# A fifth tile of at most 64 tokens: 16 second products instead of 24, and a second scatter that adds

## The chip, the cores and the metric

The kernel runs on one core of a Trainium2 chip. Its engines each work through their own list of instructions in order: TensorE (PE in the profile, its weight loads PEld), VectorE (DVE), ScalarE (ACT), GpSimd (POOL) and SyncE (SP, which here only issues DMAs). They wait for one another through semaphores. The metric is the device time of one execution in microseconds (us), the median of several runs. Before the change it is 557.7 us (three runs, 557.35 to 557.83).

## The reference

Retention over 8 batches, 8 heads, 576 positions and a head size of 64 gives `x`, 4608 tokens of 512 numbers. Each token then goes to one of eight experts:

```python
logits = xn @ en.T / tau                   # x and the expert embeddings, normalised
expert_idx = np.argmax(logits, axis=1)
gate_w = probs[np.arange(N), expert_idx]
for e in range(E):                         # E = 8, D = 512, F = 1024
    mask = expert_idx == e
    h = np.maximum(x[mask] @ w1[e], 0.0)
    out[mask] = gate_w[mask, None] * (h @ w2[e])
```

How many tokens an expert gets is known only on the chip.

## The kernel before, in words

The kernel first computes the retention and, beside it, a table that gives each expert 640 slots: five tiles of 128. `gid` holds for each slot the token whose row is gathered, `sid` the token whose row is written (a number out of range, 1e6, for an empty slot, which the scatter skips). Slots of one tile lie in an order of halves: the first of two tokens at column c of the left 64, the second at column c of the right 64. So a fifth tile with at most 64 tokens fills the first 32 columns of each half.

Numbers are float32, and each operand of the experts' products is kept as a high and a low part (`fp32r`). A product is made of three passes: high by high, high by low and low by high. From line 577 to the end of the experts all engines keep the order in which the code is written.

Each expert e from 1 to 7 goes through two stages:

- the **first products** (`x @ w1`, line 1224): seven products of blocks instead of eight, for each of four quarters i, 28 in all, in the order of the table `ORDER` (lines 1267 to 1271). A product is written (n, i). It is six matmuls of 288, 304 or 320 columns, chosen on PE by a branch on `rest[e]`, the number of tokens in the fifth tile (at most 64, at most 96, more). After each product `follow` copies and adds the bank: ACT copies `Y[i]` after n = 1, 6 and 7 into one of the five tiles `ys` (line 1248), and the next product that adds into `Y[i]` waits for that copy. `settle` turns the sums into the high part of `hs` (ACT, line 1193) and the low part (DVE, line 1186).
- the **second products** (`h @ w2`, line 1302): for each of the five tiles 24 matmuls of 512 columns (eight blocks of h times three passes) into one bank. ACT scales the bank by the gate into `ys[i]` (line 1314), and POOL scatters the 128 rows to `out` (line 1276). The fifth tile of experts 1 to 6 stands under `tc.If(rest[e] > 0)`, on PE alone: without tokens its matmuls are jumped over.

Beside these, tables of tasks (`mm1_plan`, `mm2_plan`) say after which product or tile ACT, DVE and POOL prepare what comes next: `xjoin`, `xsums`, `xhigh`, `xlow` turn the next expert's gathered tokens into its operands `xsa` and `xsb` (ACT line 446, DVE line 450), `w1hi` and `w1lo` (lines 1118 and 1121) split the weights, `w1sum` (line 1144) adds blocks of them. Three details matter here. `w1sum` of quarter 3 runs on POOL, its four additions in the first products after the sixth, and `w1hi(e, 3, False)` casts its result on ACT after the fourteenth product. The last three tasks of the second products are three copies `xturn` on ACT (line 404), which stand on ACT ahead of the fifth tile's scaling. And `ys[4]`, from which the fifth tile is scattered, is written again by ACT's copy after product (6, 2), the seventeenth of `ORDER`, which waits until the scatter has landed.

Of the kernel before, what the change touches and what calls it, by code (L numbers as in the profile page):

```python
# [18 lines left out]
P = 128  # L19
# [76 lines left out]
def retention_moe(ctx: ExitStack, tc: tile.TileContext, qk, kn, v0s, vs, w1, w2, head, cst, out):  # L96
# [262 lines left out]

    def gather(e, i, rows=N):  # L360
        a = e * CT + i
        t = xg[e, i] = raws[(2, 3, 6)[i]] if (e, rows) == (0, BEG) else raws[(i + 1) % 7]
        nc.gpsimd.indirect_dma_start(  # L363
            out=t[:, XO : XO + DM],
            out_offset=None,
            in_=xd[:rows, :],
            in_offset=bass.IndirectOffsetOnAxis(ap=gid[:, a : a + 1], axis=0),
        )

    def gather_gates(e, a0=0, a1=CT):  # L370
        if a0 == 0:
            gts[e] = mg.tile([P, CT], F32, name="gt")
        g = gts[e]
        for i in range(a0, a1):
            a = e * CT + i
            nc.gpsimd.indirect_dma_start(  # L376
                out=g[:, i : i + 1],
                out_offset=None,
                in_=gd[:, :],
                in_offset=bass.IndirectOffsetOnAxis(ap=gid[:, a : a + 1], axis=0),  # L380
            )
# [101 lines left out]
    left = keep.tile([P, NE], I32, name="left")  # L483
    rest = []

    def count_left():

        ps = psm.tile([P, 512], F32, name="m")
        nc.tensor.matmul(ps[:, :NE], ones, run, start=True, stop=True)
        nc.vector.tensor_scalar(  # L490
            out=left, in0=ps[:, :NE], scalar1=-float(CAP - P), scalar2=0.0, op0=ALU.add, op1=ALU.max
        )
        done(ps)
# [583 lines left out]
    with ExitStack() as moe:  # L1077
        mw = moe.enter_context(tc.tile_pool(name="mw", bufs=1))
        hs = mw.tile([P, 2, NF, CAP], F32R, name="hs")
        xsb = late["xsb"] = mw.tile([P, 10 * CAP], F32R, name="xsb")  # L1080
# [194 lines left out]
        def put_rows(rows_of_y, k, rows):  # L1275
            put = nc.gpsimd.indirect_dma_start(  # L1276
                out=out.rearrange("t (k n) -> (t k) n", k=k),
                out_offset=bass.IndirectOffsetOnAxis(ap=rows, axis=0),
                in_=rows_of_y,
                in_offset=None,  # L1280
                bounds_check=N * k - 1,
                oob_is_err=False,
            )
            for other in puts:
                tc.declare_no_dep(put.ins, other.ins, reason="a scatter writes other rows or other columns")
            puts.append(put)

        last_rows = []

        def mm2(e, i, tasks):  # L1290
# [5 lines left out]
            for n in range(0, DM, step):  # L1296
                ps = psm.tile([P, 512], F32, name="m")
                last = i == CT - 1 and 0 < e < NE - 1
                with tc.If(rest[e] > 0) if last else nullcontext():
                    for j, f in enumerate(SECOND):  # L1300
                        for k, (hsp, ws) in enumerate(((0, 0), (0, 1), (1, 0))):
                            nc.tensor.matmul(  # L1302
                                ps[:, :step],
                                hs[:, hsp, f, i * P : (i + 1) * P],
                                w[:, ws, f, n : n + step],
                                start=(j == 0 and k == 0),
                                stop=(j == NF - 1 and k == 2),
                            )
                            if not last and step == DM and (3 * j + k) % 8 == 7 and 3 * j + k < 23:
                                tasks((3 * j + k) // 8)  # L1310
                if last:
                    tasks(0)
                    tasks(1)
                nc.scalar.activation(y[:, n : n + step], ps[:, :step], AF.Copy, scale=gts[e][:, i : i + 1])
# [4 lines left out]
                if a < NA - 2:  # L1319
                    put_rows(*part)  # L1320
# [71 lines left out]
        for f, ps in zip(PAIRS, first):  # L1392
# [13 lines left out]
            14: [(count_left,), (xturn, 1, 3)],  # L1406
# [6 lines left out]
        for e in range(NE):  # L1413
            if e:
                plan = mm1_plan(e)
                for k, (n, i) in enumerate(ORDER, 1):
                    product(e, n, i)
                    follow(n, i)
                    if k < len(ORDER):
# [5 lines left out]
                held.pop()()  # L1425
                run_tasks(plan, len(ORDER))
# [203 lines left out]
```

## Time and profile before

| What | Value |
| --- | --- |
| Median of three runs | 557.7 us |
| The profiled execution's own time | 556.98 us |
| Its span in the profile | 555.0 us |
| PE busy, share of the span | 544.8 us, 98% |
| DVE, ACT, POOL busy | 418.5, 381.9, 231.8 us |
| Mean granted clock of TensorE | 0.995 |

The span is from the first to the last instruction of the profiled execution; some 2 us lie around it. A timeline row gives the start in us from the span's start, the duration in us, engine, line, operation, what is written and read, how many instructions are merged in it, and in brackets how long the engine sat idle before it and what ended that. A view of waits adds such idle times up by who waited for whom. A DMA that POOL issues shows as a short instruction; its landing, when the last of its 16 engines has reported, comes later and is listed separately. [...]

In the profiled execution the first products of experts 1, 6 and 7 have 304 columns, those of experts 2, 3 and 4 have 288, those of expert 5 have 320. Expert 4's second products are 96 matmuls, the fifth tile's 24 being jumped over. So the fifth tiles of experts 2 and 3 hold between 1 and 64 tokens, that of expert 4 none, those of 1, 5 and 6 more than 64.

### The profile page before, as it was taken

The numbers are of one execution on the slowest core, as the hardware profiler recorded it, in microseconds if no ns is written. First come the engines' busy times: TensorE is split into PE (matmuls) and PEld (weight loads), VectorE is DVE, ScalarE is ACT, GpSimd is POOL, SyncE is SP. The second block draws the span as 40 slices with busy tenths as digits, with TensorE's granted clock in tenths as the row PEclk, the third lists the DMA queues.
The fourth block names the chain that finished last, engine by engine and source line by source line (L and its number), as shares of the span: only waits on it lengthen the run. The fifth ranks groups of instructions, "written<-read, shape, count | busy, mean of one in ns | idle before, by whom it ended". The sixth has DMA issues, their size and how long they took to land.

```text
span 555.0 us, 13527 instructions
## 1 busy us (share of the span) xinstructions
PE 544.8 (98%) x5067; PEld 492.7 (89%) x5067; DVE 418.5 (75%) x939; ACT 381.9 (69%) x700; POOL 231.8 (42%) x233
## 2 busy tenths in 40 slices
PE   8999999999999999999999999999799999999996
PEld 8898989889998899889989988998798899889986
DVE  4757778799875878887887788788787878886810
ACT  1256455448668887888788888878878877967511
POOL 6674445554465650463065226406520650243022
PEclk9999999999999999999999999999899999999999
DMA  9999999978469576649456845837575587422211
GB/s 316 390 388 377 370 358 322 384 257 271 155 192 214 175 169 159 144 161 191 133 167 189 161 119 187 203 115 172 171 154 134 175 163 165 141 100 89 78 39 50
DMA packets 81109, 109.57 MB, mean 197 GB/s; under 512 B 42327, under 2 KB 43771, under 8 KB 81024
## 3 DMA queue, kind: packets, MB, share of 16 engines
q1 hardware_dynamic: 71920, 86.24, 54.3%
q0 software_dynamic: 7696, 19.95, 10.7%
q10 hardware_dynamic: 1408, 2.17, 1.1%
q8 instruction: 62, 1.02, 0.7%
q14 instruction: 23, 0.19, 0.1%
HBM read 80.27 MB, written 19.94 MB: 181 GB/s over the span
## 4 chain that ended last, share of the span: by engine, by line
PE 74%; DMA 10%; ACT 6%; DVE 6%; issue 3%; POOL 1%; POOLq 0%; SPq 0%; ACTq 0%; DVEq 0%
PE m L1302 16%; PE a L1224 11%; DMA out<-y,sid 9%; PE m L1224 9%; PE a L1302 9%; PE a L733 3%; PE a L460 3%; PE a L816 3%; PE m L816 2%; PE m L733 2%; PE m L460 2%; PE m L899 2%; ACT raw L411 2%; PE a L899 1%; PE m L760 1%
## 5 line engine op out<-in xcount | busy, mean ns | idle before, releaser
L1302 PE MATMUL m<-w2s,hs 128*128 128x512 f32 x600 | 138.1, 389 | 0.0
L1302 PEld LDWEIGHTS m<-w2s,hs 128*128 128x128 f32 x600 | 112.4, 188 | 23.2
L1276 POOL DMA_INDIRECT out<-y,sid x41 | 45.2, 1103 | 189.6 <-DVE wsum L1144 119.2
L1302 PE MATMUL a<-w2s,hs 128*128 128x512 f32 (+1 forms) x360 | 78.8, 375 | 0.0
L1302 PEld LDWEIGHTS a<-w2s,hs 128*128 128x128 f32 x360 | 64.2, 188 | 11.9
L363 POOL DMA_INDIRECT raw<-xd,gid x40 | 43.9, 1098 | 20.4 <-DVE sid L353 8.0
L1193 ACT ACTIVATE hs<-y 128x320 fp32r<-128x320 f32 x84 | 39.3, 474 | 17.6 <-DVE y L1244 17.3
L376 POOL DMA_INDIRECT gt<-gd,gid x40 | 40.0, 999 | 18.7 <-issue 11.8
L411 ACT COPY raw<-raw 128x1024 uint16<-128x1024 uint16 x35 | 47.4, 1355 | 0.0
L446 ACT CAST xsb<-raw 128x128 fp32r<-128x128 f32 x70 | 32.1, 458 | 21.9 <-DVE raw L429 21.4
L704 POOL TENSOR_TENSOR kt<-kt,cs 128x512 f32<-128x512 f32 x28 | 28.3, 1043 | 44.3 <-DMA kt<-kn 40.4
L1121 DVE TENSOR_TENSOR w2s<-raw,w2s 128x1024 fp32r<-128x1024 f32 x32 | 39.1, 1222 | 9.8 <-ACT w2s L1118 9.8
L1186 DVE SCALAR_TENSOR_TENSOR hs<-y,hs 128x320 fp32r<-128x320 f32 x84 | 43.3, 524 | 3.1 <-ACT hs L1193 1.1
L1224 PE MATMUL a<-xsb,w0s 128*128 128x288 f32 (+2 forms) x270 | 43.7, 302 | 0.0
L1224 PE MATMUL m<-xsb,w0s 128*128 128x288 f32 (+2 forms) x270 | 43.4, 299 | 0.0
L1224 PEld LDWEIGHTS a<-xsb,w0s 128*128 128x128 f32 x270 | 39.6, 191 | 0.0
L1224 PEld LDWEIGHTS m<-xsb,w0s 128*128 128x128 f32 x270 | 38.9, 188 | 0.0
L1244 DVE TENSOR_TENSOR y<-a,y 128x320 f32<-128x320 f32 x53 | 25.5, 485 | 14.1 <-ACT y L1248 10.9
L404 ACT COPY raw<-raw 128x1024 uint16<-128x1024 uint16 x35 | 35.4, 1045 | 0.0
L1118 ACT CAST w2s<-raw 128x1024 fp32r<-128x1024 f32 x32 | 33.4, 1043 | 2.5 <-DMA raw<-w 2.5
L422 DVE TENSOR_TENSOR raw<-raw 128x256 f32<-128x256 f32 x35 | 14.8, 424 | 25.5 <-ACT raw L411 25.5
L723 POOL TENSOR_TENSOR qkt<-qkt,gsb 128x384 f32<-128x384 f32 x32 | 31.3, 1008 | 5.8 <-issue 3.3
(259 smaller groups left out, 1183.8 us busy)
## 6 DMA issues: line engine op xcount, KB each, us to landing
raw<-w SPq DMA_DIRECT2D x64, 512.0 KB, 4.0
qkt<-qk SPq DMA_DIRECT2D x28, 576.0 KB, 7.0
xd<-y SPq DMA_DIRECT2D x36, 256.0 KB, 9.7
vt<-vs SPq DMA_DIRECT2D x7, 1152.0 KB, 12.9
kt<-kn SPq DMA_DIRECT2D x7, 1024.0 KB, 10.7
qkt<-qk ACTq DMA_DIRECT2D x4, 288.0 KB, 5.4
qkt<-qk SPq DMA_DIRECT2D x4, 288.0 KB, 5.4
out<-y,sid POOLq DMA_INDIRECT x41, 3.4
```

The lines of the kernel that those rows point to most:

```text
L363: nc.gpsimd.indirect_dma_start(out=t[:, XO : XO + DM], out_offset=None, in_=xd[:rows, :], in_offset=bass.IndirectOffsetOnAxis(ap=gid[:, a ...
L376: nc.gpsimd.indirect_dma_start(out=g[:, i : i + 1], out_offset=None, in_=gd[:, :], in_offset=bass.IndirectOffsetOnAxis(ap=gid[:, a : a + 1 ...
L404: nc.scalar.copy(far.rearrange("p (h n) -> p h n", h=2), near.rearrange("p (n h) -> p h n", h=2))
L411: nc.scalar.copy(far.bitcast(U16).rearrange("p (n h) -> p h n", h=2), near.rearrange("p (h n) -> p h n", h=2))
L446: nc.scalar.copy(hi, u)
L1118: nc.scalar.copy(hi, u)
L1121: nc.vector.tensor_tensor(out=lo, in0=u, in1=hi.bitcast(F32), op=ALU.subtract)
L1186: nc.vector.scalar_tensor_tensor(out=lo, in0=part(src), scalar=0.0, in1=hi.bitcast(F32), op0=ALU.max, op1=ALU.subtract)
L1193: nc.scalar.activation(hi, part(src), AF.Relu)
L1224: nc.tensor.matmul(ps[:, :n_cols], w[:, ws, ka, d * P : (d + 1) * P], xop(kx, xsp)[:, d, :n_cols], start=(n in (1, 2, 5) and d == 0 and k ...
L1276: put = nc.gpsimd.indirect_dma_start(out=out.rearrange("t (k n) -> (t k) n", k=k), out_offset=bass.IndirectOffsetOnAxis(ap=rows, axis=0), ...
L1302: nc.tensor.matmul(ps[:, :step], hs[:, hsp, f, i * P : (i + 1) * P], w[:, ws, f, n : n + step], start=(j == 0 and k == 0), stop=(j == NF - ...
```

## The change

For experts 1 to 6, the fifth tile gets a third case: none, at most 64 tokens, or more. With at most 64, the 32 used columns of each half are laid out again in a tile `ht`: the high parts in columns 0 to 31 and the low parts in columns 32 to 63 of the half (`both_parts`, four copies on POOL after the first products, in every one of the six experts). Each of the eight blocks of h then takes two matmuls instead of three, and the rows of the bank hold, side by side, the part from the high rows and the part from the low rows. The first scatter writes the former. A second scatter with `compute_op=ALU.add` adds the latter to the same rows of `out` (`add_low`, on POOL after the fifth product of the following expert); where the tile isn't of this kind its indices are all out of range. `low_rows` makes the two tables of indices once, on DVE.

```diff
+    def low_rows():
+        q = P // 4
+        g, r = tab[:, 0, :NE], tab[:, 1, :NE]
+        nc.vector.memset(r, BIG)
+        nc.vector.tensor_copy(g, fifth(gid))
+        for k in (0, 2):
...
+            nc.vector.tensor_copy(g[to], fifth(gid)[of])
+            nc.vector.tensor_copy(r[to], fifth(sid)[of])
...
+        nc.vector.tensor_scalar(out=sidx, in0=r, scalar1=BIG, scalar2=None, op0=ALU.add)
...
+        ht = [w0s[:, o : o + NPR * P].rearrange("p (f c) -> p f c", f=NPR) for o in (28 * P, 4096 + 28 * P)]
...
+        def both_parts():
+            for k in range(2):
+                for o, v in enumerate(ht):
+                    t = hs[:, k, NPR * o : NPR * (o + 1), (CT - 1) * P :].rearrange("p f (h c) -> p f h c", h=2)
+                    v = v.rearrange("p f (h s c) -> p f h s c", h=2, s=2)
+                    nc.gpsimd.tensor_copy(v[:, :, :, k, :], t[:, :, :, : HB // 2])
+
+        def add_low(e):
+            put_rows(ys[CT - 1], 1, sidx[:, e : e + 1], firsts[e])
...
-                with tc.If(rest[e] > 0) if last else nullcontext():
...
+                if fitted(e, i):
+                    with tc.If(rest[e] > HB) as many:
+                        passes(three)
+                    with many.Else():
+                        with tc.If(rest[e] > 0):
+                            passes(((ht, 0), (ht, 1)))
...
+                    if k == 5 and fitted(e - 1, CT - 1):
+                        add_low(e - 1)
...
+                if fitted(e, CT - 1):
+                    both_parts()
```

On POOL, from the fifth tile's scatter (out of `y_88`, with the indices `sid`) to the additions of `wsum`, this stood before, in one expert as in the others (the branches are block ends, without work):

```order
L1276 DMA out<-y_88,sid 4608x512 [waits DMASW3_49,Activation_49]
L1233 UNCONDITIONAL_BRANCH x6
L1144 TENSOR_TENSOR wsum<-raw_83 128x256 [waits DMAHW3_49,DMAHW2_49,DVE_49]
L1233 UNCONDITIONAL_BRANCH
L1144 TENSOR_TENSOR wsum<-raw_83 128x256
L1144 TENSOR_TENSOR wsum<-wsum,raw_83 128x256 [waits Pool_49]
```

At the same place of the changed kernel, and on to the end of the first products:

```order
L1308 DMA out<-y_88,sid 4608x512 [waits DMASW4_49,Activation_49]
L1263 UNCONDITIONAL_BRANCH x6
L1308 DMA out<-y_88,sidx 4608x512 [waits DMASW5_49,DMASW4_49]
L1174 TENSOR_TENSOR wsum<-raw_83 128x256 [waits DMAHW3_49,DMAHW2_49,DVE_49]
L1263 UNCONDITIONAL_BRANCH
L1174 TENSOR_TENSOR wsum<-raw_83 128x256
L1174 TENSOR_TENSOR wsum<-wsum,raw_83 128x256 [waits Pool_49]
L1263 UNCONDITIONAL_BRANCH x4
L1174 TENSOR_TENSOR wsum<-raw_83,wsum 128x256 [waits Pool_49]
L1263 UNCONDITIONAL_BRANCH x13
L1330 COPY w0s<-hs 128x8x32 [waits PE_49,Activation_49]
L1330 COPY w0s<-hs 128x8x32 [waits PE_49]
```

The adding scatter (indices `sidx`) has come between the fifth tile's scatter and the additions, and it waits on the semaphore DMASW4, which the first scatter raises when it has landed; four copies into `ht` (a part of `w0s`) have come behind the additions.

On ACT, around the cast of POOL's sums and the copy after product (6, 2) into `y_88`, the changed kernel has:

```order
L1223 ACTIVATE hs<-y_84 128x5x64 [waits DVE_49]
L1148 CAST w0s<-wsum 128x1024 [waits Pool_49]
L1263 UNCONDITIONAL_BRANCH x2
L1223 ACTIVATE hs<-y_85 128x5x64 [waits DVE_49]
L1223 ACTIVATE hs<-a_64 128x5x64 [waits PE_49]
L1278 COPY y_88<-m_69 128x320 [waits DMASW5_49,DMASW4_49,PE_49]
```

The order there is that of before; new is that the copy waits for both scatters.

## Rows read from the trace of the kernel before

**Rows 1.** Waits of PE, whole span (us in total, times, longest).

```profile
PE a L1224 <- DVE xsa L450: 1.8, 1, 1.8
PE a L1224 <- ACT xsa L446: 1.0, 1, 1.0
```

**Rows 2.** Timeline of PE: expert 2's last three tiles, expert 3's first products.

```profile
282.18 16.48 PE L1302 MATMUL m<-w2s,hs 128*128 128x512 f32 x72
298.49 1.76 PE L1224 MATMUL a<-xsa,w0s 128*128 128x288 f32 x12
...
301.67 0.96 PE L1224 MATMUL a<-xsb,w0s 128*128 128x288 f32 x6
...
314.38 1.75 PE L1224 MATMUL a<-xsb,w0s 128*128 128x288 f32 x12
```

**Rows 3.** Timeline of DVE: last low part for expert 3; split of POOL's sums.

```profile
295.98 0.41 DVE L450 TENSOR_TENSOR xsa<-raw,xsa 128x256 fp32r<-128x256 f32 x1
...
311.96 1.22 DVE L1121 TENSOR_TENSOR w0s<-wsum,w0s 128x1024 fp32r<-128x1024 f32 x1
```

**Rows 4.** Timeline of ACT in expert 3's first products.

```profile
300.17 0.42 ACT L1248 COPY y<-a 128x320 f32<-128x320 f32 x1
...
310.39 1.03 ACT L1118 CAST w0s<-wsum 128x1024 fp32r<-128x1024 f32 x1
...
312.20 0.43 ACT L1248 COPY y<-m 128x320 f32<-128x320 f32 x1
313.67 0.43 ACT L1248 COPY y<-a 128x320 f32<-128x320 f32 x1 [1.04 <-DVE hs L1186]
```

**Rows 5.** Timeline of POOL in expert 3's first products.

```profile
300.70 1.01 POOL L1276 DMA_INDIRECT out<-y,sid  x1 [0.30 <-ACT y L1248]
305.39 1.69 POOL L1144 TENSOR_TENSOR wsum<-raw 128x256 f32<-128x256 f32 x2 [3.68 <-DVE w0s L1121]
...
308.11 0.74 POOL L1144 TENSOR_TENSOR wsum<-raw,wsum 128x256 f32<-128x256 f32 x1
```

**Rows 6.** DMA issues (us to landing) of the scatters at 300.70, 350.24 and 450.39.

```profile
out<-y,sid POOLq DMA_INDIRECT x1, 6.3
...
out<-y,sid POOLq DMA_INDIRECT x1, 5.4
...
out<-y,sid POOLq DMA_INDIRECT x1, 7.8
```

**Rows 7.** Timeline of POOL: the fifth tile's scatter, stages of experts 4 and 6.

```profile
350.24 1.01 POOL L1276 DMA_INDIRECT out<-y,sid  x1 [0.31 <-ACT y L1248]
...
450.39 1.01 POOL L1276 DMA_INDIRECT out<-y,sid  x1 [0.31 <-ACT y L1248]
```

**Rows 8.** Timeline of ACT: the cast of POOL's sums, stages of experts 4 and 6.

```profile
359.83 1.03 ACT L1118 CAST wsa<-wsum 128x1024 fp32r<-128x1024 f32 x1
...
461.40 1.03 ACT L1118 CAST w0s<-wsum 128x1024 fp32r<-128x1024 f32 x1
```

**Rows 9.** Groups by line, DVE (busy us, mean ns | idle before).

```profile
L1186 DVE SCALAR_TENSOR_TENSOR hs<-y,hs 128x320 fp32r<-128x320 f32 x84 | 43.3, 524 | 3.1 <-ACT hs L1193 1.1
...
L1186 DVE SCALAR_TENSOR_TENSOR hs<-m,hs 128x320 fp32r<-128x320 f32 x16 | 7.7, 482 | 0.0
```

**Rows 10.** Timeline of DVE: two low parts beside POOL's sums, expert 6's stage.

```profile
456.53 2.01 DVE L1186 SCALAR_TENSOR_TENSOR hs<-y,hs 128x320 fp32r<-128x320 f32 x2
```

**Rows 11.** Timeline of DVE: end of expert 0's first products; small operations near the end.

```profile
173.54 0.42 DVE L1166 SCALAR_TENSOR_TENSOR hs<-m,hs 128x256 fp32r<-128x256 f32 x1 [0.72 <-ACT hs L1165]
175.73 0.42 DVE L422 TENSOR_TENSOR raw<-raw 128x256 f32<-128x256 f32 x1 [1.77 <-ACT raw L411]
...
527.61 1.52 DVE L515 TENSOR_TENSOR ovs<-ovs,ovf 128x1 f32<-128x1 f32 x8
```

**Rows 12.** All scatters' landings: us min/median/max.

```profile
DMA to landing us min/median/max: 2.2/3.4/7.8
```

**Rows 13.** Stretches of 3.4 us: busy us (count) by engine, granted clock, DMA share, GB/s.

```profile
395.40:398.80 3.40, 3.40 (x14) 3.40 (x15) 3.04 (x7) 3.40 (x5) 2.79 (x3) 0.57 0.47 148
```

More of the change, by code (lines that the diff above doesn't have):

```diff
@@ L358, in retention_moe, with fitted @@
     BEG = group_tiles(B - 3)[0] * P
+    def fitted(e, i):
+        return i == CT - 1 and 0 < e < NE - 1
     def gather(e, i, rows=N):
@@ L1273, in retention_moe, with put_rows @@
         puts = []
-        def put_rows(rows_of_y, k, rows):
+        firsts = {}
+        def put_rows(rows_of_y, k, rows, first=None):
             put = nc.gpsimd.indirect_dma_start(
@@ L1282, in put_rows @@
                 oob_is_err=False,
+                compute_op=ALU.add if first else ALU.bypass,
             )
             for other in puts:
-                tc.declare_no_dep(put.ins, other.ins, reason="a scatter writes other rows or other columns")
+                if other is not first:
+                    tc.declare_no_dep(put.ins, other.ins, reason="a scatter writes other rows or other columns")
             puts.append(put)
+            return put
         last_rows = []
+        def both_parts():
[6 more added lines that the diff above has]
+            put_rows(ys[CT - 1], 1, sidx[:, e : e + 1], firsts[e])
         def mm2(e, i, tasks):
@@ L1297, in mm2, with passes, between @@
                 ps = psm.tile([P, 512], F32, name="m")
-                last = i == CT - 1 and 0 < e < NE - 1
-                with tc.If(rest[e] > 0) if last else nullcontext():
+                def passes(forms, inner=lambda m: None):
+                    m = 0
                     for j, f in enumerate(SECOND):
-                        for k, (hsp, ws) in enumerate(((0, 0), (0, 1), (1, 0))):
+                        for rows, ws in forms:
                             nc.tensor.matmul(
                                 ps[:, :step],
-                                hs[:, hsp, f, i * P : (i + 1) * P],
+                                rows[f // NPR][:, f % NPR] if rows is ht else rows[:, f],
                                 w[:, ws, f, n : n + step],
-                                start=(j == 0 and k == 0),
-                                stop=(j == NF - 1 and k == 2),
-                            )
-                            if not last and step == DM and (3 * j + k) % 8 == 7 and 3 * j + k < 23:
-                                tasks((3 * j + k) // 8)
-                if last:
+                                start=(m == 0),
+                                stop=(m == NF * len(forms) - 1),
+                            )
+                            m += 1
+                            inner(m)
+                def between(m):
+                    if step == DM and m in (8, 16):
+                        tasks(m // 8 - 1)
+                hi, lo = (hs[:, k, :, i * P : (i + 1) * P] for k in range(2))
+                three = ((hi, 0), (hi, 1), (lo, 0))
+                if fitted(e, i):
[4 more added lines that the diff above has]
+                            passes(((ht, 0), (ht, 1)))
                     tasks(0)
                     tasks(1)
+                else:
+                    passes(three, between)
                 nc.scalar.activation(y[:, n : n + step], ps[:, :step], AF.Copy, scale=gts[e][:, i : i + 1])
@@ L1405, in retention_moe @@
             13: [(xturn, 1, 2)],
-            14: [(count_left,), (xturn, 1, 3)],
+            14: [(count_left,), (low_rows,), (xturn, 1, 3)],
         }
```

18 lines of the change are left out of this document (16 added, 2 removed).

## The prediction

> **What bounds the kernel now.** I read the waits of PE first, since PE is the engine that is busy nearly all the time. In the whole of the experts PE waits in one place only, 1.0 + 1.8 us for the operands `xsa` of expert 5 [rows 1], after the fifth tile of expert 4 that was jumped over. The reader is to see in it both that PE sets the pace and that the preparation on ACT and DVE isn't far behind: without a fifth tile's 5.4 us of cover it came last. So I read next, for a tile that will be shortened (expert 2's), PE's timeline for the pace [rows 2], then DVE's and ACT's for what stands ready when [rows 3, 4], and then POOL's with the landings of its scatters [rows 5, 6], because the adding scatter stands in POOL's order between the fifth tile's scatter and `w1sum`.
>
> **What is removed.** 72 matmuls of 512 columns start within 298.49 - 282.18 us [rows 2], which is 0.2265 us each. Eight fewer save 1.81 us, in the tiles of experts 2 and 3, the only ones with 1 to 64 tokens: 3.6 us if all of it stays.
>
> **What gives it back at once.** After expert 2's tile PE would begin expert 3's first products at 296.68 instead of 298.49. The last low part of `xsa` ends at 295.98 + 0.41 = 296.39 [rows 3], so they can begin. But the fifth product, (6, 0), adds into the bank that ACT copies after (1, 0), and that copy ends at 300.17 + 0.42 = 300.59 [rows 4]; ACT has no idle time in front of it, it comes from three `xturn` copies and the tile's scaling, and nothing in the change makes these earlier. (6, 0) started at 301.67 [rows 2]. So at most 1.08 us can be kept, some 1.0 with the latency of the semaphore, and the same holds for expert 3's tile. The possible gain is 2.0 us, not 3.6.
>
> **What the adding scatter holds up.** `add_low` waits until the first scatter has landed. POOL issued that at 300.70 [rows 5], and it landed 6.3 us later [rows 6], at 307.0. ACT's time for it is unchanged, as just said. The adding scatter then takes POOL about as long as this one, 1.01 us, and 0.30 us of issue [rows 5], so `w1sum` starts at 308.3 where it started at 305.39. Its four additions took 308.11 + 0.74 - 305.39 = 3.46 us [rows 5]; they end at 311.8. ACT's cast of their result started at 310.39 [rows 4]: 1.4 us late. Queued behind it on ACT are two high parts of `hs` and the copies after (6, 2) at 312.20 and (1, 3) at 313.67 [rows 4]; (7, 2) waits for the first of these and (6, 3) for the second. (6, 3) started at 314.38 [rows 2], 0.28 us after its copy had ended. That copy waits for low parts on DVE that stand behind the split of the cast weights, and DVE began that split at 311.96 [rows 3], 0.54 us after the cast had ended; so much of the lateness is swallowed. Anything beyond 0.28 + 0.54 = 0.8 us moves PE. In expert 3's stage that is 1.4 - 0.8 = 0.6 us later than before, and the 1.0 us gained is gone as well: +0.6.
>
> The same sum in the other stages: in expert 4's the scatter at 350.24 [rows 7] lands 5.4 us later [rows 6], `w1sum` ends at 360.4, the cast stood at 359.83 [rows 8], 0.6 us late, less 0.8: PE ends 0.2 us ahead of before instead of 1.0. In expert 6's, 450.39 [rows 7] + 7.8 [rows 6] + 1.3 + 3.46 = 462.95 against 461.40 [rows 8], 1.55 us late: +0.75, though nothing was saved there. In the stages of 2, 5 and 7 the sums end, by the same rows, no more than 0.2 us after the cast's old start: nothing. Together 0.6 - 0.2 + 0.75 = +1.15 us.
>
> **What the four copies cost.** `both_parts` runs in six experts at the change from first to second products, on a POOL that has no other work there until tile 0's scatter, a tile of 5.4 us later; its order hides the copies. What they can slow is DVE, which finishes the last low parts then and begins the next `xsums`. The trace shows no such copy. The nearest row: low parts with two operands in SBUF average 524 ns, those with one in PSUM 482 ns [rows 9], 42 ns times 84, or 3.5 us in seven stages: 0.5 us per stage for the four additions on POOL beside which they stand. In one stage two took 2.01 us [rows 10] instead of 0.96, so 1.0 is one bound; the other is 0. I take 0.3, since the copies of the high parts begin while DVE still has operands in PSUM. It reaches the end where the preparation comes last: after experts 2, 3 and 4, and through the later scatter after expert 5; four times 0.3 is +1.2, with bounds 0 and +4.
>
> **What costs nothing.** `low_rows` puts twelve small operations on DVE: eight such took 1.52 us [rows 11], so 2.3 us; DVE waited 0.72 and 1.77 us right behind that place [rows 11], which hides them; without that cover they would cost up to 2.3, once. PE's branches: PE jumped over 48 instructions after expert 4's tile and stood ready when `xsa` came [rows 1], and the shorter jumps in each product leave no gap between products [rows 2]. The adding scatter must land before ACT's copy after (6, 2). It is issued at 307.0; ACT, late itself, arrives at 313.6. Landings run from 2.2 to 7.8 us with a median of 3.4 [rows 12], so that is hidden up to 6.6. No row shows a scatter that adds.
>
> **The sum.** 1.15 + 1.2 = +2.35 us on the profiled execution's 556.98: 559.3. The median stands 0.7 above that execution, so 557.7 + 2.3 = 560.0 us.
>
> **Rivals.**
> 1. *The first scatter lands early.* If, in the new timing, it landed after 3.4 us as half of all do [rows 12], `add_low` would be done by 305.4, `w1sum` would start as before, and only ACT's copy after (1, 0) would limit: 2 x 1.0 saved, less 0 to 0.3 three times: 555.7 to 556.6. Against it: the very scatter in question was the slow one in three stages [rows 6], right behind a gather and beside the transposes that `xturn` issues. The section Anatomy of one DMA of DMA: Bandwidth & Descriptors, in the Trainium skill, speaks for this rival: about 2.0 us and the bytes at 436 GB/s, which for 128 rows of 2 KB is 2.6 us (an estimate by that page) and would make it 555.7. The trace doesn't agree, 6.3 us [rows 6], and I give it 0.2.
> 2. *The adding scatter lands late.* If reading and adding takes it beyond 6.6 us, ACT stands in front of its copy into `ys[4]` in expert 3's stage, and by the same distances within some 0.5 us in those of 4 to 6. This decides from 6.6 us on; at 9 us it would cost 2.4 us in each of four stages, 9.6 on top: 569 or more. For it speaks that 7.8 has been seen; against it that no gather stands ahead of it then. 0.08.
> 3. *PE's waits vanish into slack.* The cast's lateness could be made good by waits on ACT that I count as fixed (such as the 1.04 us in rows 4), and the copies may meet no DVE work: then 0 to +1.1, 557.7 to 558.8; or a little of the gain stays and it comes to 557. 0.2.
> 4. *The whole saving stays*, because ACT's copies come earlier than I think: 554.1. Nothing in the rows gives ACT that time. 0.04.
> 5. *The change doesn't do what it says*: the short branch isn't taken. Then nothing is saved but the waits stay: the cast's lateness alone would cost 0.6 + 0 + 0.75 and the copies their 1.2, 560.3, hardly to be told from the forecast by the time. 0.03.
>
> The forecast itself, slower by 1.2 to 5 us, has 0.45. One more thing can move any of them: right after the wait for expert 5's operands the granted clock was 0.57 on average for 3.4 us [rows 13], near the lower of TensorE's two levels (1.2 and 2.4 GHz). 14 matmuls ran there; at the upper level they take about half as long, so 1.4 us would come back if PE fell behind less there; the copies make it fall behind more.
>
> **Range and chances.** The low end takes in rival 1 whole: 555.5. The high end takes the copies at their bound of 4 instead of 1.2 and half a microsecond for the landing: 563.5. The likeliest case's own range is 558.9 to 562.7. About 0.2%, 1.1 us, is what can be told from no change here. Faster by more: 0.2 (rivals 1 and 4, but for the part of 1 that the copies eat). Within: 0.22 (rival 3 and that part). Slower: 0.58 (the forecast, 2 and 5).
>
> **What would show it.** In the changed profile: 32 matmuls that read `w0s` in second products, in two runs of 16 of 3.6 us each; a wait of PE for ACT of nearly 1 us at (6, 0) of experts 3 and 4; POOL idle until the first scatter's landing, and `w1sum` up to 3 us later in the stage than before; ACT waiting for POOL at the cast in the stages of 3, 4 and 6, and PE for ACT shortly after; longer DVE operations beside POOL's copies. It is wrong if the first scatter lands within 4 us there, if PE doesn't wait at (6, 0), if ACT's cast doesn't wait for POOL, or if the copy into `ys[4]` waits for the adding scatter.

## The result and the profile after

The changed kernel takes 564.74 us (median of five runs, 563.95 to 571.24) where the kernel before took 557.70: 1.0139 times as long, with a 95% interval of 1.0109 to 1.0169, so 7.0 us more. The forecast was 560.0 with a range of 555.5 to 563.5: the right side, too little, and outside the range. The profiled execution has a span of 562.8 us against 555.0.

Page of the changed kernel, and its waits of PE (us in total, times, longest), which answer to [rows 1]:

```profile
PE 545.8 (97%) x5051; PEld 492.6 (88%) x5051; DVE 425.5 (76%) x951; ACT 380.8 (68%) x700; POOL 267.6 (48%) x263
```

```profile
PE m L1254 <- ACT y L1278: 3.6, 3, 2.6
PE a L1254 <- DVE xsa L454: 1.8, 1, 1.8
...
PE m L1254 <- issue: 1.3, 1, 1.3
PE a L1254 <- ACT y L1278: 1.0, 2, 0.5
```

PE executes 16 matmuls fewer than the 5067 of before. The wait for `xsa` is the old one; waits for ACT's copies and 1.3 us for nothing that the profile shows are new. Where they stand is in PE's timeline of the stages of experts 3 and 4, which answers to [rows 2]:

```profile
301.68 1.06 PE L1254 MATMUL a<-xsb,w0s 128*128 128x288 f32 x6 [0.50 <-ACT y L1278]
...
308.80 1.07 PE L1254 MATMUL m<-xsb,w0s 128*128 128x288 f32 x6 [1.29 <-issue]
...
316.19 1.06 PE L1254 MATMUL m<-xsb,w0s 128*128 128x288 f32 x6 [0.75 <-ACT y L1278]
...
345.78 3.90 PE L1348 MATMUL m<-w2s,w0s 128*128 128x512 f32 x16
...
353.35 1.06 PE L1254 MATMUL a<-xsb,wsa 128*128 128x288 f32 x6 [0.49 <-ACT y L1278]
...
368.17 1.49 PE L1254 MATMUL m<-xsb,w0s 128*128 128x288 f32 x6 [2.60 <-ACT y L1278]
369.46 2.91 PE L1254 MATMUL a<-xsb,wsa 128*128 128x288 f32 x12
```

The row of 16 that reads `w0s` is expert 3's short tile. The next two rows with long waits are (6, 0) and (7, 2). The last row shows twelve matmuls in 2.9 us that took 1.75 at [rows 2]: after the wait of 2.6 us the granted clock was 0.58 for 4 us (stretch, busy time by engine, granted clock, DMA share, GB/s):

```profile
368.17:372.21 4.04, 4.04 (x19) 4.02 (x19) 3.44 (x7) 2.78 (x6) 0.00 (x0) 0.58 0.19 72
```

When each expert's second products begin, after against before (PE's timelines of both, differences worked out here), gives the loss by stage:

| Second products of expert | 1 | 2 | 3 | 4 | 5 | 6 | 7 | end of span |
| --- | --- | --- | --- | --- | --- | --- | --- | --- |
| before, us | 221.80 | 271.26 | 320.75 | 370.20 | 421.49 | 472.04 | 522.64 | 555.0 |
| after, us | 221.74 | 272.30 | 323.99 | 376.97 | 428.12 | 479.08 | 529.70 | 562.8 |
| later by, us | -0.06 | 1.04 | 3.24 | 6.77 | 6.63 | 7.04 | 7.06 | 7.8 |
| of which in this stage | -0.06 | +1.10 | +2.20 | +3.53 | -0.14 | +0.41 | +0.02 | +0.74 |

The last row counts from one column's start to the next, so the savings of the short tiles are in it. So 6.8 of 7.8 us come in the stages of experts 2, 3 and 4, though two of them begin after a shortened tile. The last 0.74 us come behind all work: the last scatter is issued 28.6 us after the start of expert 7's second products and lands 2.2 us later in both kernels, and from that landing to the end of the span 1.5 us pass before and 2.3 after. What makes this end longer, no run separates.

POOL in the same two stages, answering to [rows 5, 7], and the landings (us) of the two scatters of each stage, answering to [rows 6]:

```profile
301.73 1.01 POOL L1308 DMA_INDIRECT out<-y,sid  x1 [0.30 <-ACT y L1278]
308.85 1.61 POOL L1308 DMA_INDIRECT out<-y,sidx  x1 [6.11 <-DMA out<-y,sid]
309.92 2.02 POOL L1174 TENSOR_TENSOR wsum<-raw 128x256 f32<-128x256 f32 x2
311.32 1.30 POOL L1174 TENSOR_TENSOR wsum<-wsum,raw 128x256 f32<-128x256 f32 x1
312.70 1.35 POOL L1174 TENSOR_TENSOR wsum<-raw,wsum 128x256 f32<-128x256 f32 x1
...
360.16 1.60 POOL L1308 DMA_INDIRECT out<-y,sidx  x1 [5.76 <-DMA out<-y,sid]
361.20 3.07 POOL L1174 TENSOR_TENSOR wsum<-raw 128x256 f32<-128x256 f32 x2
363.41 1.82 POOL L1174 TENSOR_TENSOR wsum<-wsum,raw 128x256 f32<-128x256 f32 x1
365.31 0.72 POOL L1174 TENSOR_TENSOR wsum<-raw,wsum 128x256 f32<-128x256 f32 x1
```

```profile
out<-y,sid POOLq DMA_INDIRECT x1, 6.9
out<-y,sidx POOLq DMA_INDIRECT x1, 5.6
...
out<-y,sid POOLq DMA_INDIRECT x1, 6.5
out<-y,sidx POOLq DMA_INDIRECT x1, 7.1
```

And ACT, answering to [rows 4, 8]: the cast of POOL's sums in the stage of expert 2 (first as it was before, then after), and the cast and the copy after (6, 2) into `ys[4]` in those of experts 3 and 4.

```profile
260.90 1.03 ACT L1118 CAST w0s<-wsum 128x1024 fp32r<-128x1024 f32 x1
...
262.41 1.05 ACT L1148 CAST w0s<-wsum 128x1024 fp32r<-128x1024 f32 x1 [1.38 <-POOL wsum L1174]
...
314.08 1.05 ACT L1148 CAST w0s<-wsum 128x1024 fp32r<-128x1024 f32 x1 [1.93 <-POOL wsum L1174]
...
315.73 0.41 ACT L1278 COPY y<-m 128x320 f32<-128x320 f32 x1
...
366.07 1.04 ACT L1148 CAST wsa<-wsum 128x1024 fp32r<-128x1024 f32 x1 [3.79 <-POOL wsum L1174]
...
367.70 0.42 ACT L1278 COPY y<-m 128x320 f32<-128x320 f32 x1
```

One reads the chain off these: POOL stands for 6 us until the first scatter has landed, issues the adding one, makes the sums in 4.1 and 4.8 us instead of 3.46, and ACT, which had stood 1.9 and 3.8 us in front of the cast, goes on at once; PE stands 0.75 and 2.6 us soon after. The copy into `ys[4]` has no wait of its own: 308.85 + 5.6 and 360.16 + 7.1 lie before it, the latter by 0.4 us.

### The profile page after: what moved, and what is told of

It reads as the page before. It is cut to its first block, busy times and chain, and to the rows that moved or that the text cites. A ratio compares the mean times of both kernels' runs of the same rounds, so it can differ in the third digit from the quotient of the medians.

```text
span 562.8 us, 13577 instructions
## 1 busy us (share of the span) xinstructions
PE 545.8 (97%) x5051; PEld 492.6 (88%) x5051; DVE 425.5 (76%) x951; ACT 380.8 (68%) x700; POOL 267.6 (48%) x263
## 3 DMA queue, kind: packets, MB, share of 16 engines
q8 instruction: 63, 1.03, 0.8%
## 4 chain that ended last, share of the span: by engine, by line
PE 44%; ACT 17%; DVE 15%; issue 9%; DMA 9%; POOL 5%; POOLq 0%; SPq 0%; DVEq 0%; ACTq 0%
DMA out<-y,sidx 7%; PE m L1348 6%; PE a L1254 5%; ACT raw L415 4%; PE a L1348 4%; PE m L1254 4%; PE a L762 3%; PE m L762 2%; POOL out L1308 2%; ACT w2s L1148 2%; PE m L464 2%; PE a L464 2%; DVE hs L1216 2%; ACT raw L408 2%; ACT w0s L1148 2%
## 5 line engine op out<-in xcount | busy, mean ns | idle before, releaser
L1348 PE MATMUL m<-w2s,hs 128*128 128x512 f32 x552 | 127.2, 389 | 0.0
L1348 PEld LDWEIGHTS m<-w2s,hs 128*128 128x128 f32 x552 | 103.4, 188 | 21.3
L1308 POOL DMA_INDIRECT out<-y,sid x41 | 48.3, 1178 | 77.4 <-ACT y L1374 59.8
L1330 POOL CAST w0s<-hs 128x256 fp32r<-128x256 f32 x24 | 16.8, 726 | 77.6 <-ACT hs L1223 75.2
L1216 DVE SCALAR_TENSOR_TENSOR hs<-y,hs 128x320 fp32r<-128x320 f32 x84 | 49.5, 597 | 3.2 <-ACT hs L1223 1.2
L366 POOL DMA_INDIRECT raw<-xd,gid x40 | 42.7, 1067 | 19.3 <-DVE sid L353 7.7
L1254 PE MATMUL m<-xsb,w0s 128*128 128x288 f32 (+2 forms) x270 | 44.9, 304 | 4.8 <-ACT y L1278 3.4
L1274 DVE TENSOR_TENSOR y<-a,y 128x320 f32<-128x320 f32 x53 | 25.5, 485 | 12.2 <-ACT y L1278 9.3
```

The source lines that it names most:

```text
L366: nc.gpsimd.indirect_dma_start(out=t[:, XO : XO + DM], out_offset=None, in_=xd[:rows, :], in_offset=bass.IndirectOffsetOnAxis(ap=gid[:, a ...
L1216: nc.vector.scalar_tensor_tensor(out=lo, in0=part(src), scalar=0.0, in1=hi.bitcast(F32), op0=ALU.max, op1=ALU.subtract)
L1254: nc.tensor.matmul(ps[:, :n_cols], w[:, ws, ka, d * P : (d + 1) * P], xop(kx, xsp)[:, d, :n_cols], start=(n in (1, 2, 5) and d == 0 and k ...
L1308: put = nc.gpsimd.indirect_dma_start(out=out.rearrange("t (k n) -> (t k) n", k=k), out_offset=bass.IndirectOffsetOnAxis(ap=rows, axis=0), ...
L1348: nc.tensor.matmul(ps[:, :step], rows[f // NPR][:, f % NPR] if rows is ht else rows[:, f], w[:, ws, f, n : n + step], start=(m == 0), stop ...
```

## The experiments

My theory A after the result: the loss is the cast's lateness alone, by the adding scatter's place on POOL. Rivals: the copies or the short branch (B), adding as such (C), others below, each with its letter. Each kernel was compared with the kernel before on the same chip. The last column is, in the profiled execution, the time from the start of expert 0's second products to the end. It leaves out what lies ahead of them, which the change hardly touches and which differs by some 4 us between executions.

| Run | Median us | Ratio to before, 95% interval | Experts to the end, us |
| --- | --- | --- | --- |
| before | 557.70 | | 383.8 |
| after | 564.74 | 1.0139 (1.0109 to 1.0169) | 391.7 |
| e1 no adding scatter | 557.24 | 0.9983 (0.9965 to 1.0001) | 383.9 |
| e2 no copies | 563.96 | 1.0110 (1.0080 to 1.0140) | 391.2 |
| e3 sums first, tiles exchanged | 557.49 | 0.9995 (0.9977 to 1.0014) | 384.0 |
| e4 added on DVE | 558.77 | 1.0017 (1.0002 to 1.0033) | 384.9 |
| f1 24 products | 564.32 | 1.0102 (1.0060 to 1.0144) | 391.8 |
| f2 e3 with less code | 556.77 | 0.9979 (0.9961 to 0.9997) | 383.6 |
| f3 e3 with `xturn` moved | 555.05 | 0.9945 (0.9919 to 0.9971) | 381.4 |
| f4 writes instead of adds | 562.43 | 1.0071 (1.0045 to 1.0096) | 388.4 |
| g1 e3 with `xturn` moved further | 558.86 | 1.0013 (0.9997 to 1.0030) | 385.7 |
| g2 before with g1's move | 560.12 | 1.0041 (1.0021 to 1.0062) | 386.4 |
| g3 after with g1's move | 566.82 | 1.0144 (1.0108 to 1.0181) | 391.5 |
| h1 before with f3's move | 558.47 | 1.0008 (0.9987 to 1.0029) | 385.1 |
| h2 f3 again | 555.88 | 0.9962 (0.9941 to 0.9983) | 383.0 |
| h3 f3 with 24 products | 558.23 | 1.0015 (0.9998 to 1.0032) | 385.5 |

### e1: without the adding scatter

```diff
-                    if k == 5 and fitted(e - 1, CT - 1):
-                        add_low(e - 1)
```

> The adding scatters are left out, so the rows that come from the low parts of the fifth tiles of experts 2 and 3 are not brought in; the 16 products and the four copies stay. Theory A (the loss comes from POOL's chain: landing of the first scatter, 1.6 us for the adding one, then the sums beside a busy DVE, so that ACT's cast comes 1.5 to 3 us late in the stages of experts 2, 3, 4): the cast starts again 11.9 us after the start of the first products, POOL's sums take 3.5 us again, PE's waits at about 19 us into the stages go, and of 3.6 us saved some 2.0 stay: 555.6 to 557.0. Rival B (the loss comes from the short branch and the copies, through DVE and through PE's own instruction stream): still 561 or more.

Measured 557.24, 0.2 above A's range, and far from B's. No cast waits for POOL any more, and the sums of expert 3's stage are back at 3.4 us. So the loss of 7 us hangs on the adding scatter; e3 and f4 ask whether by its place or by the adding. But nothing is won either: of the 3.4 us by which the two short tiles are shorter (25.5 us for the second products instead of 27.23, twice), 2.4 are given back in expert 3's stage and 1.0 in expert 4's. PE's timeline of e1 shows where:

```profile
301.31 1.07 PE L1254 MATMUL a<-xsb,w0s 128*128 128x288 f32 x6 [0.51 <-ACT y L1278]
308.45 1.07 PE L1254 MATMUL m<-xsb,w0s 128*128 128x288 f32 x6 [1.29 <-DVE hs L1216]
...
351.45 1.06 PE L1254 MATMUL a<-xsb,wsa 128*128 128x288 f32 x6 [0.45 <-ACT y L1278]
```

The waits at (6, 0) are the ones forecast. The 1.29 us at (3, 0) are the same that the changed kernel showed as "issue"; they are f2's subject.

### e2: without the four copies

```diff
-                if fitted(e, CT - 1):
-                    both_parts()
```

> The four copies into ht are left out, so the 16 products of the short form read what lies in those columns; the adding scatter stays. Theory A: the copies cost nothing, or at most 0.5 us: 564.2 to 564.8. Rival B (the copies slow DVE at every change of stage): my forecast's 1.2 us gives 563.5, its upper bound of 4 us gives 560.7.

Measured 563.96, the experts 0.5 us shorter in one execution each. The time doesn't decide: it lies between A's range and the 563.5 of my forecast, and the interval (562.5 to 565.8) takes in both; only the bound of 4 us is out. The rows tell more. DVE beside the copies, first in e3 (with them) and then in e2 (without), at the end of expert 3's first products:

```profile
324.17 0.60 DVE L1216 SCALAR_TENSOR_TENSOR hs<-y,hs 128x320 fp32r<-128x320 f32 x1
...
326.07 0.68 DVE L1216 SCALAR_TENSOR_TENSOR hs<-y,hs 128x320 fp32r<-128x320 f32 x1
327.14 0.42 DVE L426 TENSOR_TENSOR raw<-raw 128x256 f32<-128x256 f32 x1 [0.39 <-ACT raw L415]
```

```profile
325.14 0.48 DVE L1216 SCALAR_TENSOR_TENSOR hs<-y,hs 128x320 fp32r<-128x320 f32 x1
...
327.05 0.48 DVE L1216 SCALAR_TENSOR_TENSOR hs<-y,hs 128x320 fp32r<-128x320 f32 x1
328.11 0.42 DVE L426 TENSOR_TENSOR raw<-raw 128x256 f32<-128x256 f32 x1 [0.58 <-ACT raw L415]
```

Two low parts take 0.12 and 0.20 us longer, 0.32 together, as forecast, and the same in all six experts; but DVE then waits for ACT's `xjoin` anyway, 0.39 us instead of 0.58, and part of it goes into that wait. Where PE does wait for the preparation, after the tile of expert 4 that is jumped over, the copies don't show: from the start of expert 4's second products to expert 5's first products it takes 22.98 us in e3, with the copies, and 22.96 before.

### e3: the sums first, and two tiles exchanged

```diff
-                    if k == 5 and fitted(e - 1, CT - 1):
-                        add_low(e - 1)
                     if k < len(ORDER):
                         run_tasks(plan, k)
+                    if k == 6 and fitted(e - 1, CT - 1):
+                        add_low(e - 1)
-            ya, yb, yc = ys[min(i, 1)], ys[2 + i % 3], ys[0]
+            ya, yb, yc = ys[min(i, 1)], ys[(2, 3, 2, 4)[i]], ys[0]
```

> The adding scatter stands behind POOL's sums instead of in front of them, and products (6, 2) and (6, 3) exchange the tiles that their banks are copied to, so that ys[4] is written again 3.2 us later. Theory A: the cast comes at its old time, the landing of the adding scatter (5 to 7 us after about 309 in expert 3's stage) ends before the copy after (6, 3) or at most 0.7 us late: 555.6 to 557.5. Rival C (a scatter that adds is in itself costly, by its landing in front of that copy or by the room it takes on the DMA queues): 559 to 563. Rival B: 561 or more.

Measured 557.49: A, at its upper end. The whole computation is there, and the loss is gone by the place of one instruction. (The exchange of the tiles alone can't have brought it: the copy into `ys[4]` had no wait of its own in the changed kernel.) POOL in expert 3's stage:

```profile
301.54 1.01 POOL L1308 DMA_INDIRECT out<-y,sid  x1 [0.30 <-ACT y L1278]
305.71 1.68 POOL L1174 TENSOR_TENSOR wsum<-raw 128x256 f32<-128x256 f32 x2 [3.17 <-DVE w0s L1151]
...
309.30 1.62 POOL L1308 DMA_INDIRECT out<-y,sidx  x1 [0.16 <-issue]
```

The adding scatter starts 0.45 us later than it did in the changed kernel, but now without waiting, since the landing passes behind the sums. It landed 5.1 us later, and no copy waits for it.

### e4: the low rows added on DVE

```diff
+                if fitted(e, i):
+                    for q in (0, HB):
+                        r, s = slice(q, q + P // 4), slice(q + P // 4, q + HB)
+                        nc.vector.scalar_tensor_tensor(
+                            out=y[r], in0=ps[s, :], scalar=glow[e][r], in1=y[r], op0=ALU.mult, op1=ALU.add
+                        )
                 done(ps)
```

(`add_low` and `low_rows` go; `glow` is the gate times `few`, one small operation for each expert.)

> No adding scatter and no second table of indices: VectorE adds the low rows, scaled by gate times few, to the high rows in ys[4] before the only scatter, in two operations of 32 rows by 512 for each of the six experts. Theory A: nothing waits for a landing; the two operations (0.6 to 0.7 us each) fit into the 1.06 us in which DVE waited for ACT at the start of the first products, or push its additions by 0.3 us: 555.6 to 557.5. Rival D (DVE is the tight engine there, the additions after (2, 0) and (2, 1) come late and PE waits for banks): 558 to 561.

Measured 558.77: rival D. The two operations of 32 rows take 1.53 us, where 1.2 to 1.4 were expected, and push the next addition from 301.65, in the changed kernel, to 302.78 in a stage that starts at nearly the same time:

```profile
301.22 1.53 DVE L1383 SCALAR_TENSOR_TENSOR y<-m,tab,y 32x512 f32<-32x512 f32 x2 [0.65 <-ACT y L1379]
302.78 0.49 DVE L1279 TENSOR_TENSOR y<-a,y 128x320 f32<-128x320 f32 x1
```

PE then waits for ACT again at its products 304.53 and 354.65, 0.33 us each.

### f1: the place kept, 24 products

```diff
                         with tc.If(rest[e] > 0):
-                            passes(((ht, 0), (ht, 1)))
+                            passes(three)
```

> As the changed kernel, but the tiles of 1 to 64 tokens take 24 products again (the short form is left out, so what the adding scatter brings in is no low part); copies, adding scatter and its place stay. Theory A: in the changed kernel the stages of experts 3 and 4 end by ACT's late cast, not by PE's start, so the 3.6 us saved are worth nothing there: 564.0 to 566.0. Rival E (saving and loss add up): 564.7 plus 2.0 to 3.6, so 566.7 to 568.3.

Measured 564.32: A, and E's range is outside the interval. But the profile says that it isn't quite the mechanism that I gave. Here the stages of experts 2 to 6 lose 0.6, 0.7, 1.9, 1.9 and 2.5 us, where the changed kernel's execution lost it in 2, 3 and 4; in expert 6's the first scatter landed after 7.8 us. The landings differ from execution to execution, and the loss goes where they are long. That the saving counts for nothing there is thus supported by the time, and not shown stage by stage.

### f2: less code ahead of the short tiles

```diff
-                    with many.Else():
-                        with tc.If(rest[e] > 0):
-                            passes(((ht, 0), (ht, 1)))
+                    if e > 1:
+                        with many.Else():
+                            with tc.If(rest[e] > 0):
+                                passes(((ht, 0), (ht, 1)))
```

(To e3. Expert 1's tile has more than 64 tokens, so the code left out isn't executed with these inputs.)

> As e3 (sums first, tiles exchanged), but expert 1's tile has no short form in its code; that form isn't taken there, so no executed product changes, only the length of PE's program ahead of experts 2 and 3. Theory F (the 1.2 us at product (3, 0) of expert 3 are PE waiting for its own instructions: it restarts 2.63 to 2.65 us after the begin of an instruction fetch in five runs): the wait goes or changes place and size, 556.0 to 557.5. Rival G (PE waits there for data): it stays at 1.2 us, 557.5.

In the changed kernel the trace's record of DMA packets has a transfer of 16 KB on the instruction queue that begins at 306.17 us, and PE goes on at 308.80, 2.63 later. In e1, e2, e3, e4 and f4, which execute the same matmuls, the wait at (3, 0) of expert 3 ends 2.63 to 2.65 us after the begin of such a transfer, whatever the length of the wait (0.4 to 1.3 us). In f2 PE runs through (3, 0) and waits at the next product instead:

```profile
305.29 0.96 PE L1254 MATMUL m<-xsb,w0s 128*128 128x288 f32 x6
306.61 1.05 PE L1254 MATMUL a<-xsb,wsa 128*128 128x288 f32 x6 [0.37 <-ACT raw L408]
```

again 2.63 us after one (303.98). That speaks for theory F, as far as a coincidence in seven executions and one move can: PE waits for its own instructions, though the profile names other releasers. The Trainium skill, Runtime: NRT & Kernel Launch, section Instruction fetch mechanics, states that instructions come in blocks of 16 KiB by DMA and that a taken branch out of the blocks at hand stalls until its block has come; the transfer's size in this trace agrees (16384 bytes), and that a branch is the reason here no run shows. The stage is 0.9 us shorter than e3's. The time, 556.77, lies as F has it, but its interval overlaps e3's, so the trace decides here and not the time.

### f3 and h1 to h3: ACT's queue ahead of (6, 0)

```diff
-                plan[11] += [(xturn, n + 1, 0), (xturn, n + 1, 1)]
-                plan[12].append((xturn, n + 1, 2))
+                plan[11] += [(xturn, n + 1, 0)]
...
+                plan[4] = [(xturn, n, 1)]
+                plan[8] = [(xturn, n, 2)]
                 plan[10] = [(xturn, n, 3)]
```

(f3 and h2: to e3. h1: to the kernel before. h3: to e3, with f1's edit.)

> As e3, and two of the three xturn copies that stand on ACT ahead of the fifth tile's scaling are moved behind the fourth and the eighth first product. Theory A (what is given back at (6, 0) is the queue on ACT in front of the copy after (1, 0)): PE's waits of 0.5 us at (6, 0) in the stages of experts 3 and 4 go, 0.7 us each comes back, 556.1 from 557.5. Rival H (the copies are then late for their transposes or push ACT's other copies): 557.5 to 559.

> The kernel before, with only the xturn copies moved as in f3 (behind the fourth and eighth first product). Theory A (an earlier ACT is worth something only where the tile is short; PE was full in the stages of experts 2 to 4, and the copies moved into them cost up to 0.4 us in each, as f3's stage of expert 2 shows): 557.5 to 559.5. Rival I (the moved copies alone are f3's gain): 554.5 to 555.5.

> f3 again, beside h1 and h3 on one chip: theory A 554.5 to 556.0; if f3's 555.05 was luck of its five runs, 556.5 to 557.5.

> As h2, but with 24 products in the tiles of 1 to 64 tokens (the short form is left out, so what the adding scatter brings in is no low part). Theory A (with the cast in time and ACT's queue shortened the 3.6 us of the short tiles reach the end): 2.5 to 3.6 us above h2, 557.5 to 559.5. Rival J (they are still worth little, as f1 showed for the changed kernel): within 1 us of h2.

f3 measured 555.05, 1 us less than A gave, and h2 555.88, in A's range. This is the version that beats both kernels: against the kernel before on the same chip by 1.7 us in h2 and 2.4 in f3 by the medians (2.1 and 3.1 by the ratios, both intervals below 1). h1, the same move without the change, is 558.47: not the moved copies' doing. h3 is 558.23, so the short form is worth 2.35 us there of 3.4; A said 2.5 to 3.6. In h2 the tile's scaling and the copy after (1, 0) come 0.9 and 1.5 us after the start of the first products at 295.82, where the changed kernel had 2.8 and 3.4 (ACT of h2):

```profile
296.70 0.69 ACT L1374 ACTIVATE y<-m,gt 128x512 f32<-128x512 f32 x1
297.29 0.42 ACT L1278 COPY y<-a 128x320 f32<-128x320 f32 x1
```

and PE doesn't wait at (6, 0). What is missing: the moved copies make the stages of experts 2 to 4 0.4 us longer each (22.66 us in h1, 22.26 before), and in expert 4's stage of h2 PE has a wait of 0.63 us that the profile puts down to "issue". It ends 2.43 us after the begin of a transfer on the instruction queue, not 2.63, so I leave its cause open.

### f4: the second scatter writes

```diff
-                compute_op=ALU.add if first else ALU.bypass,
+                compute_op=ALU.bypass,
```

> As the changed kernel, but the second scatter writes instead of adding (it overwrites the rows with their low parts). Theory A (the place in POOL's order costs, not the adding): the cast is as late as before, 564 to 565. Rival C (adding is the price: 1.6 us shown on POOL instead of 1.0, and longer landings): 561 to 563, and POOL's sums start 0.6 us sooner after its issue.

Measured 562.43 (two timed runs): in C's range and below A's, with an interval (559.9 to 562.8) that leaves A out. POOL of f4 in expert 3's stage:

```profile
309.15 1.00 POOL L1308 DMA_INDIRECT out<-y,sidx  x1 [6.03 <-DMA out<-y,sid]
310.17 1.44 POOL L1174 TENSOR_TENSOR wsum<-raw 128x256 f32<-128x256 f32 x2
311.57 0.73 POOL L1174 TENSOR_TENSOR wsum<-wsum,raw 128x256 f32<-128x256 f32 x1
312.38 1.35 POOL L1174 TENSOR_TENSOR wsum<-raw,wsum 128x256 f32<-128x256 f32 x1
```

C's second sign didn't come: the sums start 1.02 us after the scatter here and 1.07 in the changed kernel, so the 0.6 us more that the adding one shows isn't waited for. But behind it they take 4.13 instead of 3.56 us, and in the stages of experts 2 and 4 4.14 and 4.83 instead of 3.10 and 4.09. So adding has a price, 0.6 to 1.0 us of POOL in each of these stages (one execution each), and some 2 of the 7 us in time. The other 5 stay with a scatter that only writes: they come with its place, behind the first landing. How much of f4's time is chance of the landings isn't shown; its own second scatter landed after 7.3 us in expert 4's stage and held ACT's copy into `ys[4]` there by 0.56 us.

### g1 to g3: the copies moved further

```diff
+                plan[4] = [(xturn, n, 1)]
-                plan[10] = [(xturn, n, 3)]
+                plan[10] = [(xturn, n, 2)]
+                plan[20] = [(xturn, n, 3)]
```

(In place of f3's second part; g1 to e3, g2 to the kernel before, g3 to the changed kernel.)

> As f3, with the xturn copies put behind the fourth, tenth and twentieth first product, so that only one of them stands ahead of ACT's cast of POOL's sums. Theory A (what is left in the stages of experts 2, 3 and 4, 22.7 to 22.9 us against 22.26 before, is ACT reaching that cast 0.6 us late): each of them loses 0.3 to 0.6 us, 553.6 to 554.6. Rival H (the rest is the copies' and the sums' work on POOL beside DVE, or the transposes come late): 555 or more.

> The kernel before, with only the xturn copies moved as in g1; nothing of the change. Theory A (before, PE waits for nothing in the stages of experts 2 to 4, so an earlier ACT is worth nothing there; only the 2.8 us in front of expert 5's first products can shrink): 556.2 to 557.6. Rival I (the moved copies are the whole gain of f3, and the short tile gives none): 554.5 to 555.5.

> The changed kernel as it is, adding scatter ahead of POOL's sums, with only the xturn copies moved as in g1. Theory A (the chain begins with ACT's scaling of the fifth tile; where it is short that comes some 2.3 us sooner, and with it the scatter, its landing, the sums and the cast): the casts of experts 3 and 4, 2.7 and 3.0 us late, are nearly in time, expert 2's, whose tile ends by PE, gains 0.6 at most: 557.5 to 560. Rival J (the landing or the adding itself holds the chain, whenever it starts): 562 to 564.

All three expectations of A failed: 558.86, 560.12 and 566.82. g1 has H's time; g2 and g3 lie above their rivals' ranges too. In g2 the stages of experts 2 to 4 take 23.1 to 23.3 us instead of 22.26, and PE's timeline there has waits that neither the kernel before nor h1 has:

```profile
316.57 1.86 PE L1224 MATMUL a<-xsb,w0s 128*128 128x288 f32 x12 [0.30 <-ACT y L1248]
...
319.47 1.06 PE L1224 MATMUL a<-xsb,w0s 128*128 128x288 f32 x6 [0.26 <-ACT y L1248]
```

The second lies behind ACT's copy moved to the twentieth product (318.05 to 319.09): so late in the stage its 1.05 us on ACT reach PE. The first waits for a copy that had itself waited 1.24 us for DVE; which of the moved copies is behind that, no run separates. g3 adds one thing. ACT scaled the short tile 2.1 us earlier in the stage, but the scatter was issued only 0.2 us earlier (3.70 us after the stage's start instead of 3.91), for POOL had a gather in front of it, which itself waits for DVE:

```profile
302.80 1.33 POOL L366 DMA_INDIRECT raw<-xd,gid  x1 [0.31 <-DVE wsum L1174]
304.44 1.28 POOL L1308 DMA_INDIRECT out<-y,sid  x1 [0.30 <-issue]
```

## Why the prediction failed, step by step

- **What is removed: right.** The short tiles make the second products 1.71 us shorter (27.23 to 25.52); forecast 1.81.
- **What is given back at (6, 0): right.** PE waits 0.50 and 0.49 us there ("nearly 1 us" was foreseen); (6, 0) starts 3.86 us into expert 3's stage instead of 3.18, so 1.03 of 1.71 us are kept. f3 and h2 show the named cause, ACT's three `xturn` copies.
- **What the adding scatter holds up: the right mechanism, and the step that failed, by its size.** None of the prediction's four signs of being wrong came, so the path was as described. The term was +1.15 us; the three stages of experts 2, 3 and 4 alone lost 6.8, of which expert 2's, put at nothing, 1.10. The adding scatter was to make the casts 1.4, 0.6 and 1.55 us late in the stages of experts 3, 4 and 6 and cost 0.6 - 0.2 + 0.75. Against the old times, moved by what PE had lost before, they were late by 1.6 in expert 2's (262.41 for 260.90 - 0.06), 2.65 in expert 3's (314.08 for 310.39 + 1.04), 3.0 in expert 4's (366.07 for 359.83 + 3.24), 1.06 in expert 5's, where it cost nothing (417.70 for 409.87 + 6.77), and not by POOL in expert 6's. Two terms were too small:
  - *The landings.* I took 6.3 and 5.4 us from one execution; they were 6.9 and 6.5, in expert 2's stage 6.1 where it had been 5.5, and in expert 6's 5.3 where I had taken 7.8. f1's execution, with 7.8 there, lost its time in that stage. I read a spread as fixed numbers for each stage.
  - *The sums.* I moved them at their old 3.46 us; they took 4.13 in experts 2's and 3's stages and 4.83 in 4's. Half of that or more is the adding scatter (0.6 to 1.0 us, f4). In f4 they took 3.10, 3.56 and 4.09, so without it only expert 4's stage is clearly longer: moved to another time they meet DVE's low parts and weight split there, and those get longer too. Two low parts in expert 4's stage took 0.88 us before and 1.58 after (DVE's timelines):

```profile
360.60 0.88 DVE L1186 SCALAR_TENSOR_TENSOR hs<-y,hs 128x320 fp32r<-128x320 f32 x2
...
363.08 1.58 DVE L1216 SCALAR_TENSOR_TENSOR hs<-y,hs 128x320 fp32r<-128x320 f32 x2
```

  That POOL and DVE hold each other up is read from these durations; no run separates it. In expert 3's stage the two terms make up the whole difference: 1.4 foreseen, 0.6 from the landing and 0.67 from the sums are 2.67, measured 2.65. In expert 4's, 0.6, 1.1 and 1.37 are 3.07, measured 3.0.
- **What is swallowed: too much.** I took 0.8 us; expert 2's stage lost 1.10 of 1.57 and expert 3's 2.20 of 2.65, so it was about 0.5.
- **The clock: named, not priced.** [Rows 13] had shown what a long wait does. The 2.6 us wait of expert 4's stage was followed by 4 us at a granted clock of 0.58, near the lower of 1.2 and 2.4 GHz; 18 matmuls took 4.04 us instead of 2.4 at the pace of the others (0.133 each), 1.6 us more. It belongs in the sum wherever a wait as long as these two (2.8 and 2.6 us) is foreseen, and I foresaw none so long.
- **The copies: the wrong sum.** 0.3 us a stage on DVE was right (0.32), but nothing shows that it reaches the end: PE's wait for expert 5's operands didn't grow (e2 above). By the time, 0.5 us less in e2's execution, 1.2 isn't ruled out. If the copies cost nothing, it was luck that this term brought the forecast nearer: without it, it would have been 558.8.
- **What costs nothing:** `low_rows` was hidden: DVE did it, with the comparison that it needs, from 172.99 to 175.01 and then still waited 0.69 us for ACT. The branches weren't free: with the longer code PE waited 1.3 us once, by f2 for its instructions. In the changed kernel that lies under the late cast; in e1 and e3 it is 1.4 us of what the short tiles save.
- **The rivals.** The first scatter didn't land early, by 5.3 to 6.9 us in the stages of experts 2 to 6. The estimate worked out from the Trainium skill, DMA: Bandwidth & Descriptors, section Anatomy of one DMA, was 2.6 us; no scatter at this place bears it out, with 4.2 to 7.8 us in the kernels before and after. The adding scatter's landing held nothing in the changed kernel's execution, though by 0.4 us only; in f1's, after 7.2 us, it held ACT's copy by 0.31. The side was right. The range ended at 563.5 because its high end gave 2.8 us more to the copies and half a microsecond to the landings, and nothing to the sums. (The chances given for "slower" add up to 0.56 by the rivals, not 0.58.)

## What to carry to other kernels

An instruction that waits for a DMA's landing prices everything behind it on its engine: put it behind the work that others wait for, as e3 did. Price the landing by the spread of all such landings, and the work that is moved by what will stand beside it at its new time. A shorter job on the busiest engine is worth only what the queue behind the next release lets through: here ACT's copies had to move as well, and moved further (g1) they cost more than they gave.

## What the hardware showed that I had not expected

- An indirect scatter that adds shows mostly 1.60 to 1.63 us on POOL (46 of 60 in ten executions; the others up to 2.59), where five of f4's six that write show 1.00 (one 1.73). In the stages of experts 2 to 4 the additions behind it take 0.6 to 1.0 us longer in sum, although they start no later.
- PE's waits for instructions: seven executions show PE going on 2.63 to 2.65 us after the begin of a 16 KB transfer on the instruction queue, and the profile puts the wait down to "issue", to DVE or to ACT. The place moved by one product when code that isn't executed was left out. What makes the transfer late, I did not settle.
